# One Trainium2 core, linear attention and GeGLU block: separate places for rows of the Wo phase, and a table of shifts for the instruction order

## The chip, the core and the metric

The kernel runs on one core of a Trainium2 chip. The core has a matrix engine (PE), a vector engine (DVE), an activation engine (ACT), a general engine (POOL) and a queue engine (SP) that only issues transfers. Each takes its instructions strictly in the order of its own queue; across engines only semaphores order the work. Transfers between the chip's memory and the core's working memory are issued by SP, POOL or ACT and carried by 16 DMA engines. The metric is device time of one execution in microseconds (us), lower is better.

## The reference, cut to what matters

The input `x` is 2048 rows of 1024 numbers in bf16. A row of conditioning `c` gives six modulation rows of 1024. An adaptive layer norm feeds linear attention with 32 heads, and a second one feeds a gated MLP of width 3584.

```
mod = (silu(c) @ w_mod) -> sa, ca, ga, sb, cb, gb
h = layernorm(x) * (1 + ca) + sa
q, k, v = heads(h @ wqkv);  phi(t) = where(t > 0, t + 1, exp(t)) + 1e-6
kv = sum_s phi(k) v;  z = sum_s phi(k)
o = (phi(q) @ kv) / (phi(q) . z + 1e-6)
x = x + ga * (o @ wo)
h = layernorm(x) * (1 + cb) + sb
x = x + gb * ((gelu(h @ w_gate) * (h @ w_up)) @ w_down)
```

## The kernel before, in words

Most large products are done by a Strassen-like scheme with seven products for eight (in places nested twice), so beside the matmuls there is much vector work: sums and differences of blocks of weights (`w_unit`, `wd_sums`), of activations (`h_sum`, `h2_sums`, L1207 and L558) and of results. Every such tensor operation passes through the helper `tt_op` at L558, so L558 names many things; ACT's plain copy out of PSUM is the helper at L806.

The stages follow one another on PE. `kvq_phase` (up to 155 us in the profile) makes the first layer norm, K, V, the key-value sums and half of Q. `merge_phase` (155 to 188) finishes Q with L931, folds the key-value sums into Wo (L1021), and loads the second and third set of modulation rows (`ModSet`, loads at L567, matmuls at L575, with the Wo weights loaded at L1236). `wo_phase` (188 to 250) runs 16 row tiles of 128 rows, with 16 matmuls each (L1227). Then `gate_up(0)` (250 to 421; L1347 has 512 columns, L1358 256), `down_out(0)` (421 to 499), `gate_up(1)` and `down_out(1)` do the MLP for the two halves of the rows.

In the Wo phase, `wo_tile` takes a place from `x2_ring`, loads a block of `x` into it on SP (L1222), adds the product out of PSUM in place on DVE (L558) and stores it on POOL (L1230). `x2_ring` has 16 places in order, one for each tile, but the last two are the same memory as the first two of the second group: tiles 15 and 16 lie where tiles 7 and 8 lay. For the first eight tiles, `ln2_stats` takes the mean and variance on DVE (L636, L638), ACT makes the reciprocal root (L649, L650), and `ln2_xhat` writes the normalized block to a place of `xh2_ring` on DVE (L1168), and POOL stores it to a scratch tensor (L1170, `xhs`). `xh2_ring` has three places in turn. After four blocks a transposed load on SP (L1162) brings 512 rows back as the operand of the MLP, ACT or DVE modulates it (L1205, L1207), and DVE forms the block differences (`h2_steps`). The other eight tiles are normalized later, during `gate_up(0)`, by `late_norm` on ACT (L1184, L1185, L1189), with a reload at L1180. `down_out` starts with differences of gate results on DVE (L1537, L1538).

All memory places are fixed by hand (`at(offset in KB, shape, type)`), and phases share memory. `h12[1]` (operands of Q) covers 136 to 152 KB, `Sab` and the last three-place group of `wm2_ring` lie from 152 on, the gate results `A22` cover 130 to 144 KB, and the f32 copies of `gate_up` (`f32_ring`) 158 to 170.

The order of instructions is made by a planner in the kernel's source. `te`, `ve`, `ac`, `gp` and `sy` do not emit; they record operations with their dependences (`Plan.add`, at the grain of 16 bytes of memory and of a PSUM bank). `Plan.order` keeps PE in the recorded order and sorts the other four engines by due times, found in alternating forward and backward sweeps with a cost for each operation (`cost`, `sweep`); the best forward sweep gives the order. `Plan.issue` then emits the operations in that order. Semaphore waits follow from the dependences. Transfers of SP and ACT take eight semaphores in turn, those of POOL another eight, so a transfer also waits until the one eight places before it in that sequence has landed.

Of the kernel before, what the change touches and what calls it, by code (L numbers as in the profile page):

```python
# [11 lines left out]
BF16 = mybir.dt.bfloat16  # L12
F16 = mybir.dt.float16
# [2 lines left out]

ACT_TABLE_LN_EXP = 6
GA_SCALE = 1024.0

class Op:  # L20
    __slots__ = ("extra", "eng", "fn", "args", "kw", "line", "cost", "bytes", "table", "preds", "succs", "early", "late", "due", "ready", "wait", "lat", "needs",
# [2 lines left out]
class Plan:  # L24
# [225 lines left out]
    def order(self):  # L250


        best = None

        def forward(look):
            nonlocal best
            t = self.sweep(False, lambda o: (o.due, o.n), look)
            if best is None or t < best[0]:
                best = (t, sorted((op.start, op.n) for op in self.ops))

        for op in self.ops:
            op.due = op.n
        for i in range(2 * self.ROUNDS):
            forward(i >= self.ROUNDS)
            old = [op.due for op in self.ops] if i else None
            for op in self.ops:
                op.due = op.start
            t = self.sweep(True, lambda o: (-o.due, -o.n))
            for op in self.ops:
                op.due = best[0] * (1 - op.done / max(t, best[0]))  # L270
                if old:
                    op.due += self.KEEP * (old[op.n] - op.due)
            for a, b in [*zip(self.chain, self.chain[1:]), *self.pairs]:
                b.due = max(a.due, b.due)
        return [self.ops[n] for _, n in best[1]]

    def issue(self):
        with self.tc.manual_schedule():
# [9 lines left out]
def kernel(  # L288
# [19 lines left out]
    S, D = x_in.shape  # L308
# [77 lines left out]
    def at(off, shape, dt):  # L386
        return Ring(off, shape, dt, 1)()
# [122 lines left out]
    sub_a = [at(76 + 3.5 * j, [NPR // 2, HB], F16) for j in range(3)]  # L510
    sub_b = [at(189 + 3.5 * j, [NPR // 2, HB], F16) for j in range(4)]
    x2_ring = Ring(207, [D], BF16, 6)
    x2_ring.slots += Ring(191, [D], BF16, 4).slots + Ring(176, [D], BF16, 4).slots + Ring(191, [D], BF16, 2).slots
    x2e_ring = Ring(144, [D], BF16, 3)
    xhe_ring = Ring(150, [D], F16, 3)
    junk = at(156, [D], BF16)
    xh2_ring = Ring(199, [D], F16, 3)

    psT = Banks(0, 3)
    psM = Banks(6, 7)  # L520
# [497 lines left out]
    def wp_step(g):  # L1018
        psw = psW.pair()
        for h in range(2):  # L1020
            te.matmul(psw[:, h, :], lhsT=KVbdT[:, g, :], rhs=Wog[:, g, h * NW:(h + 1) * NW], start=True, stop=True)  # L1021
        ac.activation(out=Wp[:, g, :], in_=psw.rearrange("p h n -> p (h n)"), func=AF.Copy, scale=1.0 / GA_SCALE)

# [209 lines left out]
    def merge_phase(stages):  # L1233
# [4 lines left out]
        for i, stage in enumerate(stages):  # L1238
# [10 lines left out]
            if i == 3 + 1:  # L1249
                kv_transposes()  # L1250
                ms1.columns()
                ms1.spread(0, garow, GA_SCALE)
                for g in range(KD):
# [533 lines left out]
```

## Time and profile before

| what | value |
|---|---|
| three runs | 755.2, 755.6, 759.06 us; median 755.6 |
| profiled execution | 753.23 us, span 751.4 us |
| PE / DVE / ACT / POOL busy | 728.5 / 623.4 / 427.3 / 96.7 us |
| bytes read from and written to memory | 116.00 and 32.37 MB, 197 GB/s over the span |
| transfers of the SP and ACT queues | 50.9% and 0.8% of 16 DMA engines |
| transfers of POOL's queue | 13.4% |
| granted TensorE clock | 1.0 in all slices |

The span goes from the first to the last instruction, and the execution's time has 1.8 us around it. In the chain that ended last, PE holds 52% of the span, DVE 9%, ACT 5%, DMA 2%. A matmul's recorded duration includes the time until its results are out; the next one starts before that, so busy shares of PE overstate its work. In the views of waits, an engine's name with a q (SPq) is its queue, and a line such as "X <- Y: 4.0, 3, 1.9" says that X stood 4.0 us in total for Y, 3 times, 1.9 us at the longest. Lines and idle times of DVE and ACT matter only where PE or a transfer waits for them in the end.

### The profile page before, as it was taken

What the parts mean: (1) busy time and instruction counts of PE and PEld (TensorE: products, weight loads), DVE (VectorE), ACT (ScalarE), POOL (GpSimd) and SP (SyncE); (2) the same over time, 40 slices, a digit from 0 to 9 for tenths busy, and PEclk for the clock granted to TensorE, in tenths of its full rate; (3) what the DMA queues carried; (4) which work ended last, traced back from release to release, by engine and by line L of the source; (5) the groups of instructions that cost most, each with busy time, mean ns of one, the idle gap of its engine ahead of it and who ended that gap; (6) DMA issues with size and microseconds to landing.
All of it is one profiled execution on the core that took longest, in us unless ns stands there. A gap on an engine that the chain in (4) does not pass through costs nothing.

```text
span 751.4 us, 11753 instructions
## 1 busy us (share of the span) xinstructions
PE 728.5 (97%) x4228; PEld 395.9 (53%) x4242; DVE 623.4 (83%) x1386; ACT 427.3 (57%) x772; POOL 96.7 (13%) x171
## 2 busy tenths in 40 slices
PE   5999999999989899999999999999999999999997
PEld 2444545444434455555555486645555555548664
DVE  6898997778976899999999789587787888888763
ACT  3674666669311879999878710017777777741000
POOL 2354842000122002112100000010000000000000
PEclk9999999999999999999999999999999999999999
DMA  9878966896879935468761988652332313399832
GB/s 303 312 197 246 284 173 127 307 351 177 242 249 230 297 126 170 153 218 275 256 191 63 282 260 257 228 182 88 110 101 68 113 57 113 104 275 288 278 114 74
DMA packets 141723, 149.15 MB, mean 198 GB/s; under 512 B 33760, under 2 KB 121312, under 8 KB 140384
## 3 DMA queue, kind: packets, MB, share of 16 engines
q1 hardware_dynamic: 125408, 116.14, 50.9%
q0 software_dynamic: 13904, 30.15, 13.4%
q10 hardware_dynamic: 2352, 2.10, 0.8%
q8 instruction: 33, 0.54, 0.3%
q14 instruction: 26, 0.21, 0.1%
HBM read 116.00 MB, written 32.37 MB: 197 GB/s over the span
## 4 chain that ended last, share of the span: by engine, by line
PE 52%; DVE 9%; ACT 5%; issue 2%; DMA 2%; SPq 0%; DVEq 0%; ACTq 0%
PE psum L1347 23%; PE psum L1559 13%; PE psum L1603 9%; PE psum L1358 8%; DVE mem L558 7%; DMA mem<-xhs 2%; ACT mem L806 2%; DVE psum L558 1%; ACT mem L1205 1%; PE psum L1227 0%; ACT mem L1430 0%; ACT mem L1184 0%; ACT mem L1189 0%; ACT mem L1420 0%; ACT psum L1403 0%
## 5 line engine op out<-in xcount | busy, mean ns | idle before, releaser
L558 DVE TENSOR_TENSOR mem<-mem 128x512 f16<-128x512 f16 (+10 forms) x753 | 332.0, 486 | 21.6 <-ACT mem L806 6.7
L1347 PE MATMUL psum<-mem 128*128 128x512 f16 x1144 | 282.7, 379 | 1.2 <-ACT psum L1403 0.8
L806 ACT ACTIVATE mem<-psum 128x512 f32<-128x512 f32 (+3 forms) x310 | 162.6, 553 | 111.7 <-PE psum L1603 50.5
L558 DVE TENSOR_TENSOR mem<-psum,mem 128x512 f16<-128x512 f32 (+4 forms) x204 | 154.9, 764 | 42.5 <-ACT mem L806 18.3
L1347 PEld LDWEIGHTS <-mem 128*128 128x128 f16 (+1 forms) x1144 | 111.7, 98 | 92.4 <-issue 3.0
L1358 PE MATMUL psum<-mem 128*128 128x256 f16 x742 | 115.9, 272 | 2.1 <-DVE psum L558 1.8
L1358 PEld LDWEIGHTS <-mem 128*128 128x128 f16 (+1 forms) x742 | 72.5, 98 | 59.7 <-issue 8.8
L1559 PE MATMUL psum<-mem 128*128 128x512 f16 (+2 forms) x458 | 99.0, 372 | 0.7 <-DVE mem L558 0.5
L1559 PEld LDWEIGHTS <-mem 128*128 128x128 f16 x462 | 45.2, 98 | 49.9 <-issue 0.7
L1603 PE MATMUL psum<-mem 128*128 128x256 f16 (+1 forms) x588 | 66.2, 273 | 0.0
L1603 PEld LDWEIGHTS <-mem 128*128 128x128 f16 x588 | 57.5, 98 | 9.2
L861 PE MATMUL psum<-mem 128*128 128x512 f16 (+1 forms) x272 | 61.6, 379 | 0.4
L558 DVE TENSOR_TENSOR psum<-psum,mem 128x256 f32<-128x256 f32 x106 | 45.3, 428 | 19.4 <-ACT mem L806 19.2
L1227 PE MATMUL psum<-mem 128*128 128x512 f16 x256 | 56.2, 379 | 4.0 <-DVE mem L558 4.0
L1403 ACT ACTIVATE psum<-psum 128x512 f32<-128x512 f32 x56 | 33.1, 592 | 37.7 <-PE psum L1347 28.2
L931 PE MATMUL psum<-mem 128*128 128x512 f16 x224 | 51.3, 379 | 1.3 <-ACT mem L901 1.0
L861 PEld LDWEIGHTS <-mem 128*128 128x128 f16 x280 | 27.0, 98 | 31.2
L1227 PEld LDWEIGHTS <-mem 128*128 128x128 bf16 x256 | 24.8, 98 | 34.9 <-issue 5.7
L1420 ACT ACTIVATE mem<-psum 128x512 f16<-128x512 f32 x56 | 33.1, 597 | 12.9 <-PE psum L1347 12.6
L931 PEld LDWEIGHTS <-mem 128*128 128x128 f16 (+1 forms) x224 | 21.5, 97 | 28.6 <-issue 3.8
L1430 ACT ACTIVATE mem<-mem 128x512 f16<-128x512 f16 x56 | 35.3, 634 | 1.2 <-DVE mem L558 0.7
L636 DVE BATCH_NORM_STATS2 mem<-mem 128x6 f32<-128x512 bf16 x48 | 31.0, 673 | 1.9 <-DMA mem<-in_A_x_dram 1.8
(126 smaller groups left out, 522.1 us busy)
## 6 DMA issues: line engine op xcount, KB each, us to landing
mem<-in_B_w_gate_dram SPq DMA_DIRECT2D x14, 1024.0 KB, 6.8
mem<-in_B_w_up_dram SPq DMA_DIRECT2D x14, 1024.0 KB, 7.4
mem<-in_w_mod_dram SPq DMA_DIRECT2D x24, 512.0 KB, 7.4
mem<-us SPq DMA_DIRECT2D x24, 448.0 KB, 8.1
mem<-ts SPq DMA_DIRECT2D x6, 1792.0 KB, 8.3
mem<-in_A_x_dram SPq DMA_DIRECT2D x32, 256.0 KB, 4.4
ts<-in_B_w_down_dram POOLq DMA_DIRECT2D x28, 256.0 KB, 8.5
us<-mem POOLq DMA_DIRECT2D x7, 768.0 KB, 5.6
```

What stands on the lines that cost most here:

```text
L558: ve.tensor_tensor(out=out, in0=a, in1=b, op=op)
L806: ac.activation(out=t, in_=ps, func=AF.Copy)
L861: te.matmul(ps, lhsT=A[:, k, i * P:(i + 1) * P], rhs=B[:, k, :], start=(start and k == 0), stop=(k == KH - 1), skip_group_check=True)
L931: te.matmul(o, lhsT=W[:, k, (j0 + i) * P:(j0 + i + 1) * P], rhs=h_form(a, k), start=(start and k == 0), stop=(k == KH - 1), skip_group_che ...
L1227: te.matmul(psw[:, half, :], lhsT=pqT[b][:, g, tl * P:(tl + 1) * P], rhs=Wp[:, g, half * NW:(half + 1) * NW], start=(g == 0), stop=(g == K ...
L1347: te.matmul(ps, lhsT=a[:, k, e, :], rhs=b[:, k, :], start=(start and k == 0), stop=(k == KH - 1), skip_group_check=True)
L1358: te.matmul(ps, lhsT=self.x[a][:, k, :], rhs=self.y[y][:, k, :], start=(start and k == 0), stop=(k == KH // 2 - 1), skip_group_check=True)
L1403: ac.activation(out=z, in_=x, func=AF.Copy)
L1420: ac.activation(out=o, in_=ps, func=AF.Gelu_apprx_tanh)
L1430: ac.activation(out=o, in_=o, func=AF.Gelu_apprx_tanh)
L1559: te.matmul(psm[:, q, c], lhsT=A[:, i, q * P:(q + 1) * P], rhs=wt[:, i, c], start=(start and i == 0), stop=(i == NPR - 1), skip_group_chec ...
L1603: te.matmul(ps[:, q, :], lhsT=a[:, k, q * P:(q + 1) * P], rhs=y[:, k, :], start=(start and q == 0 and k == 0), stop=(k == NPR // 2 - 1), s ...
```

## The change

It has two parts. The places: `xh2_ring` moves from 199 KB with three places to 156 KB with eight, one for each block normalized in the Wo phase; the last two places of `x2_ring` move from 191 KB (shared with tiles 7 and 8) to 136 KB. The planner's dependences follow from this, and with them the order that it finds.

The order: a table `SHIFTS` holds, for each of DVE, ACT, POOL and SP, one number per operation. The new `refine` takes the planner's order of each engine and replaces it by a permutation: the operation at position i becomes the one that stood at i plus the i-th number (a word such as z3 stands for three zeros). PE has no table and keeps its order. It then merges the five queues into one sequence by earliest start, with an operation's results counted as there after its latency, 4000 ns more for transfers. That sequence is emitted; it decides on each engine's order only through the table, and also on the turn in which transfers take their semaphores.

```diff
+SHIFTS = {
+    "DVE": (
+        "z1 7 8 -2 7 7 -2 -1 1 -7 4 -8 4 -8 -1 z1 -9 2 -1 -1 1 2 2 -3 2 4 1 1 2 2 2 2 2 -11 7 7 -11 16 16 -4 -2 -1 13 1 "
...
+    "SP": (
+        "2 2 -2 -2 2 -1 -1 z4 1 6 -2 z1 -2 z1 -2 1 -2 z1 2 -1 -1 2 z1 -2 1 4 z1 -3 z1 -2 2 -1 -1 1 -1 5 6 4 -3 -3 -1 12 "
...
-        return [self.ops[n] for _, n in best[1]]
+        return self.refine([self.ops[n] for _, n in best[1]])
+
+    def refine(self, ops):
+
+        seqs = {e: [op for op in ops if op.eng == e] for e in self.engines}
+        for e, text in SHIFTS.items():
+            shifts = []
+            for word in text.split():
+                shifts += [0] * int(word[1:]) if word[0] == "z" else [int(word)]
+            assert sorted(i + d for i, d in enumerate(shifts)) == list(range(len(seqs[e])))
+            seqs[e] = [seqs[e][i + d] for i, d in enumerate(shifts)]
+        at, free, done, out = dict.fromkeys(seqs, 0), dict.fromkeys(seqs, 0.0), {}, []
+        while len(out) < len(ops):
+            heads = []
+            for e, seq in seqs.items():
+                if at[e] < len(seq) and all(p in done for p in seq[at[e]].preds):
+                    op = seq[at[e]]
+                    heads.append((max([free[e], *(done[p] for p in op.preds)]), op.n))
+            start, n = min(heads)
+            op = self.ops[n]
+            at[op.eng] += 1
+            free[op.eng] = start + op.cost
+            done[n] = start + op.lat + (4000 if op.bytes else 0)
+            out.append(op)
+        return out
...
-    x2_ring.slots += Ring(191, [D], BF16, 4).slots + Ring(176, [D], BF16, 4).slots + Ring(191, [D], BF16, 2).slots
+    for at_x2, n in ((191, 4), (176, 4), (136, 2)):
+        x2_ring.slots += Ring(at_x2, [D], BF16, n).slots
...
-    xh2_ring = Ring(199, [D], F16, 3)
+    xh2_ring = Ring(156, [D], F16, 8)
```

## The prediction, made before the changed kernel ran

> **What bounds the kernel now.** I read the page's head first, then the busy time by stage, then who PE waits for, and last the timelines around those waits.
>
> ```profile
> span 751.4 us, 11753 instructions
> PE 728.5 (97%) x4228; PEld 395.9 (53%) x4242; DVE 623.4 (83%) x1386; ACT 427.3 (57%) x772; POOL 96.7 (13%) x171
> ```
>
> PE is the bound, but 97% overstates it: a 512-column matmul is recorded with 379 ns while the next one starts 216 ns after it (256 columns: 109 ns; 128: 57 ns). The 4242 planned matmuls at these pitches (2555 x 0.216, 1358 x 0.109, 168 x 0.057, and 144 small ones at 0.062) make 718 us. So 751.4 - 718 = 33 us of the span is not matmul work, and only that can shrink, because the PE order is untouched. 3.5 us of it is the tail after the last matmul.
>
> Stages: start, K/V and Q, merge, Wo, first gate/up pass, its down projection, second gate/up pass, the rest. Columns: length, PE, PE loads, DVE, ACT, POOL busy (instructions), clock, DMA share, GB/s.
>
> ```profile
> 0.00:34.00 34.00, 24.24 (x150) 11.32 (x152) 25.36 (x82) 15.13 (x27) 10.80 (x38) 1.00 0.98 336
> 34.00:155.00 121.00, 120.53 (x660) 58.17 (x671) 106.89 (x220) 78.12 (x100) 47.69 (x69) 1.00 0.82 221
> 155.00:188.00 33.00, 31.71 (x210) 13.95 (x204) 25.56 (x50) 26.69 (x32) 0.31 (x1) 1.00 0.76 254
> 188.00:250.00 62.00, 57.99 (x294) 25.68 (x287) 47.00 (x78) 17.11 (x35) 12.60 (x23) 1.00 0.89 244
> 250.00:421.00 171.00, 168.12 (x942) 91.76 (x941) 161.17 (x415) 147.62 (x298) 19.61 (x32) 1.00 0.60 196
> ...
> 499.00:664.00 165.00, 164.60 (x946) 92.24 (x945) 135.85 (x334) 119.67 (x247) 1.42 (x2) 1.00 0.33 102
> ```
>
> Clock 1.00 throughout. From start distances minus pitches the lost time is 13.7 us in the start, 0.1 in K/V and Q, 2.1 in merge, 4.9 in Wo, 6.8 in the first gate/up pass, 0 in its down projection, 1.6 in the second pass, 0.7 after, and the tail. The two gate/up passes are a control: 576 + 364 matmuls take 170.6 us, 568 + 378 take 165.2, and the pitches give 163.8 and 163.6. The first differs by its neighbours: DVE is 94% busy (161.17 of 171), in the second 82%.
>
> ```profile
> PE psum L670 <- DVE mem L657: 5.8, 1, 5.8
> PE psum L1227 <- DVE mem L558: 4.0, 3, 1.9
> PE psum L707 <- DMA mem<-in_c_dram: 2.2, 1, 2.2
> PE psum L1358 <- DVE psum L558: 1.8, 7, 0.4
> PE psum L931 <- ACT mem L901: 1.0, 1, 1.0
> PE psum L1347 <- ACT psum L1403: 0.8, 3, 0.4
> ```
>
> The column is total us, times, longest. PE waits for evictions that stand late in the DVE or ACT queue, not for DVE or ACT as a whole.
>
> **Part 1: the places, Wo (term A).** DVE is stuck here:
>
> ```profile
> 212.46 0.55 DVE L1168 TENSOR_SCALAR mem<-mem 128x1024 f16<-128x1024 bf16 x1 [4.02 <-DMA xhs<-mem]
> ...
> 242.88 0.42 DVE L558 TENSOR_TENSOR mem<-mem 128x512 f16<-128x512 f16 x1 [4.16 <-ACT mem L1205]
> 244.30 1.09 DVE L558 TENSOR_TENSOR mem<-mem 128x512 f16<-128x512 f16 x3 [0.99 <-ACT mem L1205]
> ```
>
> At 212.46 the normalization of the fourth row block waited 4.02 us for the store of the first to leave one of three shared places. Behind it on DVE stood the PSUM add of a Wo tile, so PE stood 2.03 us at 216.05 and 0.53 at 220.04. Eight places for eight blocks take the wait away. At 246.58 PE stood 1.94 us because a Wo add was queued behind gate/up subtractions that waited 4.16 and 0.99 us for ACT L1205, and L1205 waited for a transposed load:
>
> ```profile
> SPq L1222 <- DMA x2s<-mem: 19.2, 1, 19.2
> ```
>
> SP held the x load of the 15th tile 19.2 us, until the slot of the 7th was stored, and the transposed load stood behind it: issued 227.49, landed 241.22 (13.73 us), though its fourth block had landed at 218.13. With places of their own the two last x loads need no slot of tiles 7 and 8, and the new SP order has both transposed loads ahead of them. The load can go 9.4 us earlier, and DVE has the Wo add ahead of the last subtractions. What is late next is the second transposed load (last store landed 235.64; it went at 237.4, landed 246.9), which gates only modulations that gate/up reads after 250. A is bounded by 0 and -4.9; I take -4.3 (two kinds of waits named, both removed). The new waits: the new places need the last readers of Q operands and modulation rows (PE, 188.3 at the latest; first block needed near 201), and later f32 copies and gate results there need stores that land by 235.6 and 257.3, before 250 and well before 300. Cost nothing; without that cover it would be the few us by which a store is late.
>
> **Part 2: the order.** Every instruction of DVE, ACT, POOL and SP keeps its work; 1280 of 1373, 654 of 765, 129 of 150 and 173 of 204 stand elsewhere.
>
> Term B, first gate/up pass. ACT now does second-half modulations between evictions PE waits for:
>
> ```profile
> 415.68 0.84 ACT L1205 ACTIVATE mem<-mem 128x512 f16<-128x512 f16 x1
> 416.39 0.62 ACT L806 ACTIVATE mem<-psum 128x512 f32<-128x512 f32 x1
> 416.86 0.85 ACT L1205 ACTIVATE mem<-mem 128x512 f16<-128x512 f16 x1
> ```
>
> Six such L1205 stand ahead of the last ACT result that this pass needs; in the new order one: 5 x 0.82 = 4.1 us leave. On DVE, from the first shared h2 sum to the last result needed, 409 instructions become 400 (188.3 to 183.8 us of recorded durations): six of twelve down-projection differences (L1537, L1538, 0.685 each = 4.1) go behind it, into a stage with DVE 62 of 78 busy. So ACT and DVE get about 4 us more slack each where 6.8 us is lost. If the pass then behaves like the second one it loses 1.6; I take a loss of 2.1, so B = -4.7, bounds 0 and -6.8.
>
> Term C, merge. PE stood 1.18 at 171.65 for L901, which ran behind L891, which waited for a product with the Wo weights (issued 155.27, landed 166.11). SP now issues that load after one row of the last modulation set, not four: at least 3 x 1.27 (landing distance of such rows) sooner. C = -1.2, bounds 0 and -2.1.
>
> Term D, start. c goes third, the first x block fourth (was second): two or three issue steps of 0.47 late, 0.9 to 1.4. Against it, the weight rows PE waits for next (landed 12.89) have the same bytes ahead of them. D = +0.3, bounds -0.7 and +1.4.
>
> Term E, second pass: eight of the 25 L1537/L1538 ahead go behind it, 8 x 0.685 = 5.5 us more DVE slack. E = -1.2, bounds -1.6 and +1.
>
> Term F, the rest has almost nothing to lose and can only be hurt; +0.4, bounds 0 and +2. DVE 83%, POOL 13% hide moved work.
>
> Sum: -4.3 - 4.7 - 1.2 + 0.3 - 1.2 + 0.4 = -10.7, span 740.7. The profiled execution was 753.23 for a span of 751.4; the median of three is 755.6 (755.2 to 759.06), 2.4 above. On that footing 755.6 - 10.7 = 744.9; I say 745.
>
> The Trainium skill, "Perfetto Trace Analysis", section "Identifying the Most-Contended Engine", holds matmul busy time to be a poor measure; the 379 against 216 ns agrees. By idle time alone Wo would offer 4.0 instead of 4.9.
>
> **The rivals.**
>
> Slower, one mechanism: DVE instructions now stand before their DMA data. The new merge of queues reckons a DMA done 4.0 us after its own cost, while weight-sum loads take a median of 8.1 (ts) and modulation rows 7.4. DVE queues in order: a sum placed by that timetable holds the queue 8.1 - 4.0 = 4.1 us. With five such chunks in the first pass that is 20.5 us against 9.8 us idle there: +10.7, no B, other terms as above: 755.6 - 6.0 + 10.7 = 760.3. It turns the sign from four chunks on (4 x 4.1 - 9.8 = 6.6 against 6.0). A sister is the last two modulation rows, now behind den loads on SP: issued near 175, needed near 186; at the longest latency seen (13.42) 2 us late, which alone doesn't turn the sign. Against: SP, not DVE, waited for most such loads' places (L1073, L1074: 47.6 and 45.4 us). Chance 0.12. The skill's "DMA: Bandwidth & Descriptors", section "Anatomy of one DMA — SWDGE (gpsimd) path", would give 512 KB about 2.0 + 1.2 = 3.2 us, an estimate by which both dangers vanish; the rows' 7.4 decide against it.
>
> No change: DVE's 161 of 171 is work, not order, and Wo's gain returns as waits in the pass: 755. For: 94%. Against: 4 us really leave. Chance 0.08.
>
> Only the places act: A alone, 755.6 - 4.3 = 751.3. Chance 0.10.
>
> All waits go: -4.9 - 6.8 - 2.1 - 0.7 - 1.6 = -16.1, 739.5. Chance 0.15.
>
> **How the numbers follow.** My forecast, 742 to 750, has 0.55. The range 739.5 to 754 leaves out the slower case and most of no change, about 0.17. 0.5% (3.8 us) is about what this kernel's measurement can tell: faster below 751.8. Faster: 0.55 + 0.15 + 0.08 of the places' case = 0.78; same 0.02 + 0.08 = 0.10; slower 0.12.
>
> **What will show it.** Span near 741. DVE L1168 waits for no xhs store; SP L1222 for no x2s store; the first xhs transposed load issued near 218; L1227 waits for DVE under 0.5 instead of 4.0 (A). First gate/up pass 166 us instead of 170.6, with fewer L1358/L1347 waits (B). L931 on L901 under 0.5 (C). First L670 between 8.2 and 9.6 (D). I am wrong if the first pass stays at 170, if L575 waits for its w_mod rows near 186, or if DVE waits on ts or w_down loads.

## The result and the profile after

The changed kernel takes 744.15 us (median of four runs, 743.69 to 745.04); the kernel before, run beside it, 755.4 us. The ratio is 0.9847, with a 95% interval of 0.9808 to 0.9887. The forecast was 745.0. The profiled execution took 743.69 us. Of the 39 runs of the kernel before that stand beside the experiments, 26 had a mean granted clock under 1.0 (down to 0.993) and a median of 756.77 us, the 13 at 1.0 one of 753.27, while all ten runs of the changed kernel (here and in e9) had 1.0: about 2 us of the 11 between the medians go with the clock, and the profiled executions, both at 1.0, differ by 9.5 us. In the changed kernel every line of the phases stands 97 further down: L558 is now L655, L1227 is L1324, L1347 is L1444, L1162 is L1259.

The head of the page:

```profile
span 741.9 us, 11731 instructions
PE 726.5 (98%) x4242; PEld 396.1 (53%) x4242; DVE 626.3 (84%) x1386; ACT 422.8 (57%) x772; POOL 96.7 (13%) x171
```

Busy times have hardly moved; 9.5 us of span have gone. So the time came out of gaps. The busy times by stage show where (start, merge, Wo, first gate/up pass, second pass; columns as before: length, PE, PE loads, DVE, ACT, POOL busy with instructions, clock, DMA share, GB/s):

```profile
0.00:34.50 34.50, 24.42 (x150) 11.25 (x151) 24.60 (x82) 12.86 (x23) 10.77 (x38) 1.00 0.98 337
...
156.00:187.30 31.30, 31.27 (x210) 14.02 (x206) 27.28 (x53) 27.73 (x33) 0.31 (x1) 1.00 0.78 266
187.30:245.00 57.70, 57.70 (x291) 25.74 (x284) 48.80 (x81) 17.84 (x36) 11.50 (x21) 1.00 0.96 263
245.00:412.00 167.00, 165.95 (x943) 91.84 (x942) 156.39 (x401) 140.58 (x287) 21.43 (x34) 1.00 0.61 195
...
490.30:654.70 164.40, 164.14 (x946) 92.39 (x945) 133.10 (x330) 114.63 (x243) 2.84 (x4) 1.00 0.35 110
```

PE is recorded as busy through the whole Wo phase (57.70 of 57.70, against 57.99 of 62.00 before); by the distances between starts, below, 0.62 us are still lost in it. From its first matmul to the first of the down projection the first pass takes 166.8 us, where it took 170.8 before. The clock is 1.00 in all these rows. Waits of PE (total us, times, longest):

```profile
PE psum L804 <- DMA mem<-in_c_dram: 4.2, 1, 4.2
PE psum L767 <- DVE mem L754: 4.2, 1, 4.2
PE psum L782 <- DVE mem L775: 1.0, 1, 1.0
PE psum L1455 <- DVE psum L655: 0.7, 3, 0.3
```

The Wo matmul (L1227, now L1324), which had headed the list together with the start's own wait, is gone from it; what is left at the head belongs to the start. Of the chain that ended last, PE now holds 85% where it held 52%:

```profile
PE 85%; DVE 7%; ACT 4%; issue 2%; DMA 1%; SPq 0%; DVEq 0%; ACTq 0%
```

The lost PE time by stage, worked out as in the prediction (distances between starts of matmuls, less their pitches), puts numbers on it. Start and K/V are given together, since they differ between runs of one order. The first column is a median in us, then the ratio to the kernel before with its interval, then lost us by stage in the profiled execution:

| kernel | median | ratio | start, K/V, Q | merge | Wo | pass 1 | down 1 | pass 2 |
|---|---|---|---|---|---|---|---|---|
| before | 755.4 | 1 | 13.85 | 2.06 | 4.87 | 6.75 | 0.00 | 1.60 |
| changed | 744.15 | 0.9847 (0.9808–0.9887) | 14.59 | 0.48 | 0.62 | 2.77 | 0.23 | 0.91 |
| e1_planner_order | 754.14 | 0.9998 (0.9971–1.0025) | 14.61 | 2.77 | 0.38 | 8.38 | 0.00 | 2.50 |
| e2_old_order_new_places | 748.96 | 0.9918 (0.9887–0.9948) | 14.58 | 2.15 | 0.38 | 6.74 | 0.00 | 1.60 |
| e3_table_until_gate | 747.32 | 0.9919 (0.9892–0.9945) | 14.36 | 0.48 | 0.62 | 5.85 | 0.00 | 1.60 |
| e4_table_from_gate | 744.05 | 0.9877 (0.9836–0.9917) | 14.38 | 1.82 | 0.38 | 2.65 | 0.23 | 0.90 |
| e5_old_start | 743.0 | 0.982 (0.9786–0.9853) | 13.91 | 0.48 | 0.62 | 2.73 | 0.22 | 0.88 |
| e6_moves_back | 745.03 | 0.9848 (0.9806–0.9891) | 14.75 | 0.48 | 0.62 | 4.56 | 0.00 | 0.88 |
| e7_pool_back_gate | 748.68 | 0.99 (0.9863–0.9938) | 14.24 | 0.48 | 0.62 | 7.83 | 0.22 | 0.88 |
| e8_xh2_places_only | 749.1 | 0.9901 (0.9866–0.9936) | 14.40 | 1.95 | 0.38 | 6.70 | 0.00 | 1.57 |
| e9_changed_again | 744.29 | 0.9837 (0.9806–0.9867) | 14.38 | 0.48 | 0.62 | 2.71 | 0.22 | 0.88 |
| e10_old_start_again | 743.45 | 0.9826 (0.9795–0.9856) | 14.53 | 0.48 | 1.05 | 2.73 | 0.23 | 0.88 |
| e11_wo_load_late | 745.07 | 0.9847 (0.9814–0.9879) | 14.51 | 2.14 | 0.62 | 3.63 | 0.23 | 1.19 |
| e12_act_back | 744.46 | 0.9839 (0.9807–0.9871) | 14.79 | 0.48 | 0.62 | 3.17 | 0.22 | 1.17 |

The experiments ran in three groups (e1 to e4, e5 to e8, e9 to e12), each beside runs of the kernel before with medians of 753.71, 756.77 and 756.77 us. That kernel alone differs by a few us from run to run, so across groups the ratios and the stages are compared, not the medians. The interval of a ratio is 0.003 to 0.004 to either side; the stages resolve more, and where two kernels have the same order in a stage they mostly agree within 0.1 us there, with a few stages 0.2 to 0.4 off (the old merge, 1.82 in e4 to 2.15 in e2, Wo in e10, the second pass in e11 and e12) and one 0.9 off (the first pass in e11).

### The profile page after: what moved, and what is told of

It is laid out like the page before. It is cut to its first block, busy times and chain, and to the rows that moved or that the text cites. A ratio compares the mean times of both kernels' runs of the same rounds, so it can differ in the third digit from the quotient of the medians.

```text
span 741.9 us, 11731 instructions
## 1 busy us (share of the span) xinstructions
PE 726.5 (98%) x4242; PEld 396.1 (53%) x4242; DVE 626.3 (84%) x1386; ACT 422.8 (57%) x772; POOL 96.7 (13%) x171
## 4 chain that ended last, share of the span: by engine, by line
PE 85%; DVE 7%; ACT 4%; issue 2%; DMA 1%; SPq 0%; DVEq 0%; ACTq 0%
PE psum L1444 26%; PE psum L1656 13%; PE psum L1455 9%; PE psum L958 8%; PE psum L1324 7%; PE psum L1028 7%; PE psum L1700 6%; DVE mem L655 5%; PE psum L1057 4%; PE psum L782 2%; ACT mem L903 2%; PE psum L1072 1%; DMA mem<-in_w_mod_dram 1%; DVE psum L655 1%; ACT mem L1281 1%
## 5 line engine op out<-in xcount | busy, mean ns | idle before, releaser
L655 DVE TENSOR_TENSOR mem<-mem 128x512 f16<-128x512 f16 (+13 forms) x753 | 336.6, 488 | 15.2 <-ACT mem L1302 4.1
L1444 PE MATMUL psum<-mem 128*128 128x512 f16 x1144 | 282.3, 379 | 0.6 <-ACT psum L1500 0.2
L655 DVE TENSOR_TENSOR mem<-psum,mem 128x512 f16<-128x512 f32 (+4 forms) x204 | 155.0, 765 | 36.8 <-PE psum L1656 10.1
L1444 PEld LDWEIGHTS <-mem 128*128 128x128 f16 (+1 forms) x1144 | 111.8, 98 | 91.4 <-issue 1.6
L655 DVE TENSOR_TENSOR psum<-psum,mem 128x256 f32<-128x256 f32 x106 | 45.5, 430 | 32.4 <-ACT mem L903 31.6
L1324 PE MATMUL psum<-mem 128*128 128x512 f16 x256 | 55.9, 379 | 0.0
L1324 PEld LDWEIGHTS <-mem 128*128 128x128 bf16 x256 | 24.8, 98 | 30.4 <-issue 0.4
```

Source lines behind the costliest of these rows:

```text
L655: ve.tensor_tensor(out=out, in0=a, in1=b, op=op)
L1324: te.matmul(psw[:, half, :], lhsT=pqT[b][:, g, tl * P:(tl + 1) * P], rhs=Wp[:, g, half * NW:(half + 1) * NW], start=(g == 0), stop=(g == K ...
L1444: te.matmul(ps, lhsT=a[:, k, e, :], rhs=b[:, k, :], start=(start and k == 0), stop=(k == KH - 1), skip_group_check=True)
```

## The experiments

The order of an engine can be chosen freely through the table, so most experiments are the changed kernel with another table: "old order" means the permutation that gives exactly the order of before. Of such tables the first words that differ are shown.

**e1: the places without a table.**

```diff
-        return self.refine([self.ops[n] for _, n in best[1]])
+        return [self.ops[n] for _, n in best[1]]
```

> The new places, without the table: the planner's own order on them is emitted. Theory (the places alone remove the Wo waits, 4.3 us): 755.4 - 4.3 = 751.1 us, Wo loses 0.6 us or less instead of 4.9, the first gate/up pass still loses about 6.8. Rival (the planner, given other dependences, finds another order, and this gives the gain back elsewhere): Wo loses 0.6 too, but merge and the first pass lose 4 more together, 755 us.

The ratio is 0.9998: nothing gained. Wo does lose its gaps (0.38 instead of 4.87), but merge, first and second pass lose 0.7, 1.6 and 0.9 us more than before. The planner answers the new places with another order: 582 of 1373 operations on DVE and 121 of 765 on ACT stand elsewhere. One place of the merge shows what that does (DVE, then PE):

```profile
170.14 1.90 DVE L655 TENSOR_TENSOR mem<-mem 128x1024 f16<-128x1024 bf16 x3 [2.77 <-DMA mem<-in_A_wo_dram]
```
```profile
170.89 0.59 PE L1118 MATMUL psum<-mem 128*128 128x512 f16 x2 [2.06 <-DVE mem L655]
```

DVE stood 2.77 us for the Wo weights with a product that PE needs behind it, and PE stood 2.06. What made the first and second pass dearer was not traced. The rival was right in kind: the planner gives the gain back, about 2.3 us in merge and first pass together (forecast 4) and 0.9 in the second pass. Removing a wait of 4 us was worth nothing as long as the order was free to change with it.

**e2: the places, with the old order.**

```diff
     "DVE": (
-        "z1 7 8 -2 7 7 -2 -1 1 -7 4 -8 4 -8 -1 z1 -9 2 -1 -1 1 2 2 -3 2 4 1 1 2 2 2 2 2 -11 7 7 -11 16 16 -4 -2 -1 13 1 "
...
```

(The new table starts with zeros on all four engines.)

> The new places, and a table that gives DVE, ACT, POOL and SP exactly the order of the kernel before. Theory (the waits in Wo were waits for places): Wo loses 0.1 to 0.6 us instead of 4.9, everything else as before: 750.7 to 751.1 us. Rival (the new order of SP and DVE in Wo removed them): the two waits at 216 and 220 go, the one at 247 stays, Wo loses 2 or more, 753 us or more.

The Wo phase drops from 4.87 to 0.38, every other stage stays as before within what runs differ by. So 4.5 us are the places' own. e2 has, beside the old order of each engine, the new merge of the five queues, and so another turn of the semaphores of the transfers; since its other stages lose what they lost before, that merge by itself changes nothing that can be seen, and it was the order through which e1 lost the gain. The median, 748.96, lies under the 750.7 to 751.1 that were expected, which counted from 755.4; beside it the kernel before had 753.71, and the difference, 4.75, is close to the 4.3 to 4.7 expected.

**e3 and e4: which half of the new order.** e3 has the new order up to the first matmul of the first pass and the old one after, e4 the reverse. Both have the new places.

```diff
e3, DVE from position 416:
-        -2 -1 1 20 z1 1 3 4 z1 -4 z1 2
+        -7 -3 -2 z4 1 -1 1 -1 z1
e4, DVE up to position 445:
-        7 8 -2 7 7 -2 -1 1 -7 4 -8 4
+        z12
```

> The order of the changed kernel up to the first gate/up pass, from there the order of the kernel before (new places in both). Theory (what the first pass gains is its own order): merge and Wo lose 1.1 us together as in the changed kernel, the first pass loses 6 to 7, the second 1.6: 744.15 + 4.0 + 0.7 - 0.2 = 748.7 us. Rival (the pass gains since its operands come earlier): first pass about 3, 745 us.

> The reverse: the order of the kernel before up to the first gate/up pass, the changed kernel's from there (new places in both). Theory: Wo loses 0.6 or less by the places, merge 2.1 as before, the first pass 2.8 as in the changed kernel: 744.15 + 1.6 - 0.7 = 745 us. Rival (the pass needs what the table did ahead of it): the first pass loses 5 or more, 747.5 us or more.

With the new order only before the pass (e3) the merge has its gain (0.48), and the first pass falls from 6.74 (e2) to 5.85, a little under the 6 to 7 of the theory: 0.9 us come with the new order ahead of the pass (that it is by operands which are ready earlier was not traced). With the new order only from the pass on (e4) the pass falls from 6.74 to 2.65, no worse than the 2.77 of the changed kernel. So the order inside the pass gives all of its gain by itself, and the 0.9 us do not come on top of it. The 0.7 us of the second pass follow the same switch: 1.60 in e3, 0.90 in e4.

**e5 and e10: the old start.** The old order up to the merge, the new one from there. Both runs are one and the same kernel.

```diff
DVE up to position 284:
-        7 8 -2 7 7 -2 -1 1 -7 4 -8 4
+        z12
```

> The old order of the four engines until merge begins, the new order from there. Theory (the new start is dearer by the 0.3 + 0.4 us that the prediction gave it): start and K/V lose 13.9 us instead of 14.6, 743.4 us. Rival (the start is the same within what runs differ by): 14.4 to 14.6, 744.1 us.

> The old order up to the merge and the new one from there (e5_old_start once more), beside the changed kernel. Theory (term D: the new start costs 0.3 to 1 us): ratio 0.0005 to 0.003 below that of the changed kernel, and PE loses under 14.1 us in start and K/V here, over 14.3 there. Rival (the two starts are the same, what was seen is the difference between runs): ratio within 0.001 and both losses within 0.3 us of each other, or the other way round.

> The changed kernel, unaltered, beside the next three on one chip. Both theories: a ratio between 0.981 and 0.989, about 744 us; lost PE time by stage as in its first profile within 0.5 us (start with K/V 14.6, merge 0.5, Wo 0.6, first gate/up pass 2.8).

e5 looked 1 us better than the changed kernel. Beside the changed kernel on one chip it was 743.45 to 744.29, ratios 0.9826 and 0.9837 with intervals that overlap almost whole, and its start with K/V lost 14.53 us, the changed one's 14.38. Over all runs the old start lost 13.85 to 14.58 us and the new one 14.24 to 14.79. The price of the new start, if there is one, is below what these runs can tell; no version better than the changed kernel is shown.

**e6 and e12: the moved work.** e6 puts the six differences (DVE, L1537/L1538 of before) and the five modulations (ACT, L1205 of before) back ahead of the last result that the first pass needs; e12 only the five modulations.

```diff
e6, DVE from position 762:
-        10 3 1 10 2 -47 -25 9 -33 5 10 -6
+        9 9 2 z1 7 8 z1 -49 -27 7 -35 3
e6 and e12, ACT from position 440:
-        3 1 5 6 6 -4 -1 6 z1 5 5 8
+        -1 2 z1 3 3 4 4 -6 -3 4 -2 3
```

> The changed kernel, but the six down-projection differences on DVE (L1537, L1538 of before) and the five modulations on ACT (L1205) that it moved behind the first gate/up pass are put back ahead of the instructions they preceded before. Theory (term B: the pass gains since this work left it): first pass loses 6 us or more instead of 2.8, 747.5 us. Rival (it gains by the fine order of what stays): 3.5 us or less, 744.8 us or less.

> The changed kernel with only the five modulations (ACT) put back ahead of the last result that the first gate/up pass needs; the six differences on DVE stay behind it. e6_moves_back, with both back, lost 4.56 us in this pass instead of 2.77. Theory (DVE is the tighter of the two): the pass loses under 3.3 us and the time is within 0.6 us of the changed kernel. Rival (ACT is the tighter one): the pass loses 4.0 us or more and the time rises by 1.2 us or more.

With both back the first pass loses 4.56 instead of 2.77. That lies between what the theory asked for (6 or more) and what the rival did (3.5 or less): the moved work is a part of the gain. In the list of PE's waits of e6 this group has grown; in the changed kernel it is 0.7, 3 times, 0.3 at the longest:

```profile
PE psum L1454 <- DVE psum L654: 1.1, 4, 0.5
```

With only ACT's back it loses 3.17. So ACT's five are worth 0.4 and, by difference, DVE's six the other 1.4: 1.8 together. DVE was the tighter engine. In e6 the down projection loses nothing; wherever the six differences go behind the pass, it loses 0.2. That is the price of the move.

**e7: POOL alone back.** The 34 instructions of POOL in the first pass return to the relative order of before. DVE, ACT and SP keep the new one.

```diff
POOL from position 108:
-        3 -3 5 2 z1 3 z1 3 7 5 -9 1
+        -2 z4 3 z2 -3 z3
```

> The changed kernel, but POOL's 34 instructions during the first gate/up pass are in the relative order of before (stores of weight sums L1085 and L1087 and of normalized rows L1190, roots L1187). Theory (POOL is 13% busy and costs nothing): first pass loses 2.8, 744.1 us. Rival (a store or a root that stands late on POOL holds DVE's queue, as in the slower rival of the prediction): first pass loses 5 or more, 746.5 us or more, with a DVE wait on POOL or on a us or ts store of 2 us or more.

The first pass loses 7.83 us instead of 2.77, more than before, though POOL is busy for 13% of the span. The waits in this pass (244 to 415 us) that the changed kernel's list doesn't have:

```profile
DVE mem L654 <- DMA us<-mem: 2.4, 1, 2.4
...
PE psum L1454 <- DVE mem L1282: 2.4, 1, 2.4
...
DVE mem L1284 <- POOL mem L1283: 1.2, 2, 0.8
```

How they hang together is seen on the timelines of e7, POOL first:

```profile
314.99 0.54 POOL L1286 DMA_DIRECT2D xhs<-mem  x1 [7.03 <-ACT mem L1285]
315.54 0.57 POOL L1283 TENSOR_TENSOR mem<-mem 128x1 f32<-128x1 f32 x1
316.06 0.58 POOL L1181 DMA_DIRECT2D us<-mem  x1
```
```profile
320.51 1.36 DVE L654 TENSOR_TENSOR mem<-mem 128x512 f16<-128x512 bf16 x3 [2.43 <-DMA us<-mem]
...
322.59 0.42 DVE L654 TENSOR_TENSOR psum<-psum,mem 128x256 f32<-128x256 f32 x1
```
```profile
323.53 0.58 ACT L1499 ACTIVATE psum<-psum 128x512 f32<-128x512 f32 x1 [2.78 <-PE psum L1454]
```
```profile
323.07 0.38 PE L1454 MATMUL psum<-mem 128*128 128x256 f16 x2 [2.36 <-DVE mem L1282]
```

POOL waited 7.03 us for ACT with the store of a normalized block, and the store of weight sums (`us`) stood behind it until 316.06. DVE's next weight sum needs the place that this store frees: it waited 2.43 us, with evictions out of PSUM behind it (the one at 322.59 among them), and PE stood 2.36. In the changed kernel the same store does not stand behind an `xhs` store (POOL):

```profile
310.23 0.58 POOL L1182 DMA_DIRECT2D us<-mem  x1 [9.46 <-DVE mem L655]
```

It went 5.8 us earlier, as soon as its data was there. So the rival was right here, and the theory that POOL costs nothing was wrong.

The stop is half of the 5.1 us that e7 loses more. By the distances between starts of matmuls against the changed kernel's, 2.5 us are the stop itself, 0.9 lie in three short waits just before it (293 to 318 us), and 1.7 come after it: from 323.8 on, 512-column matmuls start 427 ns apart instead of 216, and the granted clock is down (e7, columns as in the tables by stage):

```profile
322.00:324.00 2.00, 0.93 (x5) 0.54 (x5) 2.00 (x6) 0.47 (x1) 0.85 (x1) 0.91 1.05 393
324.00:326.00 2.00, 2.00 (x8) 0.99 (x7) 1.93 (x7) 1.49 (x4) 0.08 (x1) 0.50 0.10 33
326.00:328.00 2.00, 2.00 (x9) 0.78 (x8) 1.86 (x6) 0.67 (x2) 0.00 (x0) 0.74 0.03 8
```

At 328 it is 1.00 again. That makes about 3.4 us at half the clock. The run doesn't say that POOL's old order is a bad one: it says that it doesn't fit DVE's new one.

**e8: only the eight places of the normalized blocks.** The two last places of `x2_ring` are shared as before; old order.

```diff
-    for at_x2, n in ((191, 4), (176, 4), (136, 2)):
-        x2_ring.slots += Ring(at_x2, [D], BF16, n).slots
+    x2_ring.slots += Ring(191, [D], BF16, 4).slots + Ring(176, [D], BF16, 4).slots + Ring(191, [D], BF16, 2).slots
```

> Eight places for the normalized rows, the last two x places shared as before, and exactly the order of the kernel before. Theory (two kinds of waits): the two waits at 216 and 220 go, the one at 247 (SP behind the x slot) stays: Wo loses 2 to 2.5 us, 751 us. Rival (one chain: with DVE earlier the slot is free earlier too): Wo loses 0.6 or less, 749 us, the same as with both places.

Wo loses 0.38, as with all the new places (e2). SP still waits for the store of an earlier tile, and the transposed load still stands behind it (the wait, then SP's timeline):

```profile
SPq L1278 <- DMA x2s<-mem: 16.8, 1, 16.8
```
```profile
223.88 8.19 SPq L1218 DMA_TRANSPOSE mem<-xhs  x1
```

The load goes 3.6 us earlier than before (227.49), and that was enough. With it DVE's stop is gone: the store of the fourth block leaves POOL at 209.71, where it left at 213.30 before, also 3.6 us earlier. The third stop of the Wo phase, which the prediction laid to the shared `x2` places, went with the first two. This is what the rival had said. The reverse, separate `x2` places alone, was not run, so what they would be worth without the others is open.

**e11: the Wo load late.** On SP, three more weight rows of the last modulation set go ahead of the load of the Wo weights, as before.

```diff
SP from position 48:
-        5 1 -3 4 -1 -4
+        2 -2 -1 2 3 -2
```

> The changed kernel with one move on SP: three more weight rows of the last modulation set go ahead of the load of the Wo weights, as before. Those rows stood until 155.86 us for a place that PE frees, so the load goes at about 157 instead of 147.4. Theory (term C: the early load is what took the merge's wait away): PE stands again for products with the Wo weights, the merge loses 1.5 to 3.5 us instead of 0.5, and the time rises by 1 to 3 us. Rival (the merge's gain is from the order on DVE and ACT): the merge stays within 0.4 us of 0.5 and the time within 0.5 us.

The load's issue in the changed kernel, and in e11:

```profile
147.38 0.48 SPq L1333 DMA_DIRECT2D mem<-in_A_wo_dram  x1
```
```profile
157.10 0.43 SPq L1333 DMA_DIRECT2D mem<-in_A_wo_dram  x1
```

What follows in e11 on DVE and PE:

```profile
169.26 0.69 DVE L655 TENSOR_TENSOR mem<-mem 128x1024 f16<-128x1024 bf16 x1 [2.01 <-DMA mem<-in_A_wo_dram]
```
```profile
170.00 0.59 PE L1118 MATMUL psum<-mem 128*128 128x512 f16 x2 [1.30 <-DVE mem L655]
```

DVE waits 2.01 us for the weights, PE 1.30 for DVE. The merge loses 2.14 instead of 0.48: the early load is the whole of the merge's gain. The span is 3.0 us longer than that of e9 (744.6 against 741.6), of which 0.9 lie in the first pass; there DVE waits 0.92 us for a load of `w_up` at 252.20 and PE 0.69 for DVE at 259.80, and whether this follows from the late load was not tried. The median is 0.8 above, just under the 1 to 3 us of the theory.

## Why the prediction was right, and where it wasn't

The total was right: 745.0 against 744.15, and a span of 741.9 where the sum gave 740.7. The sum said -10.7; the two profiled spans differ by -9.5. That the total came within 0.9 us of the median is partly luck: the sum took off 1.2 us too much, and the footing put the median 2.4 us above the profiled execution, as in the kernel before, where the changed kernel's is 0.5 above. The two errors work against each other. By the terms of the sum:

- **A, the places: -4.3 forecast, -4.25 measured.** The size was right and half of the reasoning was not needed. "Two kinds of waits named, both removed": e8 removes one of them and gets it all. The shared `x2` places held SP for 16.8 us in e8 and cost PE nothing; the transposed load was late enough to stop PE only because DVE's stop at the fourth block had made everything behind it 3.6 us late. The signs named ahead did come: L1324 off the list of waits, no L1319 waiting for `x2s`, the first transposed load at 216.86 (forecast near 218). Two of those three would have been seen without being a cause.
- **B, first pass: -4.7 forecast, -3.98 measured.** This is the mis-sized term, and its mechanism covers less than half. "About 4 us more slack each" was worth 1.8 us (e6): 0.4 on ACT (e12), by difference 1.4 on DVE. The other 2.2 us or so lie in the rest of the order inside the pass, since that order gives all of the gain with the old one ahead of it (e4). No experiment takes this rest apart; e7 shows that the order of POOL's stores and DVE's weight sums must fit in it. The pass did not behave "like the second one": it loses 2.77, not 2.1.
- **C, merge: -1.2 forecast, -1.58 measured.** The step was right. The load went earlier by 7.9 us, not by the "3 x 1.27" of the sum, since the rows it had stood behind were waiting for places that PE frees; but PE could gain no more than it had lost.
- **D and F: +0.3 and +0.4 forecast, +0.39 and +0.58 measured** (start; K/V and first down projection). Of these only the 0.23 of the down projection holds in further runs, and it belongs to the six moved differences (e6). The rest is within what runs of one order differ by. The first matmul of L670 came at 8.60 us, as D had it (8.2 to 9.6).
- **E, second pass: -1.2 forecast, -0.69 measured.** Its moves were not tried by themselves; e3 and e4 show that the gain goes with the order from the first pass on.

Of the rivals, the slower one did not come: no DVE instruction in the first pass of the changed kernel waits for a transfer, and the merge loses 0.48 with the last modulation rows where the forecast feared them. Its kind of trouble is real, though. With one engine's queue out of step DVE stops for 2.4 us in e7, and the pass loses 5.1 us more, 1.7 of them by the clock after the stop. Against the danger of late modulation rows the prediction also worked out 3.2 us by a formula of the skill; the section that it names fits that formula to transfers which POOL issues, while these rows are issued by SP, so their 7.4 us don't speak against it. "Only the places act", 751.3, is a case that has two answers, depending on who orders: 0.9918 with the old order (e2) and 0.9998 with the planner's own (e1). The prediction took the places' gain as given. The part ahead of it had named a planner that sorts by due times, and the prediction did not ask what that planner does with new dependences. The table is what keeps the gain of the places, apart from what it gains itself.

## What to carry to other kernels

When a planner or scheduler sets the order, a freed wait is not worth what the trace shows until the order is held fixed: price it twice, once in the old order and once in the one that the planner then makes. When one engine's order is changed, go through every queue that hands places to it, a nearly idle one too, and ask what each store stands behind. Of several waits that end at one place remove one and look again, because the others may only have been late through it.

## What the runs showed of the hardware that had not been expected

- A stop of PE can cost more than its own length. After the stop of 2.5 us in e7 the granted clock is down to 0.50 for about 3.4 us, which costs 1.7 us more. After the stops of 2.03 and 1.94 us in the Wo phase of the kernel before, and of 2.2 us in the merge of e1, the clock stays at 1.00 in the profiled executions. What decides was not tried. An estimate from e7: one such stretch lowers the mean clock of a run by 0.5 x 3.4 / 750 = 0.002. The runs of the kernel before, with means down to 0.993, would then have up to three of them; that its stops bring them on fits the record (e2, without the stops of the Wo phase, has 1.0 in nine runs of ten and 0.999 in one) but isn't shown, since of the kernel before one execution alone was profiled.
- The first 12 us or more run at half the rate, though the rows of the start say 1.00. In the kernel before, 128-column matmuls start 106 or 107 ns apart until 12.1 us, and 55 or 56 after that; in the changed kernel they are still 107 ns apart at 13.3 us.
- A transposed load from memory holds SP for different times with the same kind of work: 9.09 us for the first one in the kernel before, 5.93 in the changed one, 5.70 in e2 and 8.19 in e8, for 512 rows each time. What sets it was not tried.
- The lost time of the start differs by up to 0.7 us between runs with one and the same order there (13.85 to 14.58 with the old one), while later stages mostly repeat within 0.1 us. A change of the start worth less than that can't be told from a few profiles.
